# Four tokens to a partition for q and k of the first two units, and the second unit's norms ahead of its gates

## The chip, the cores and the metric

One core of one Trainium2 chip runs the whole kernel. The metric is device time in microseconds of one execution; the median over several runs is compared. The engines are TensorE (PE; PEld is its weight load), VectorE (DVE), ScalarE (ACT), GpSimd (POOL) and SyncE (SP), each with an instruction stream of its own that runs in order; they wait for one another on semaphores. Loads that change float32 to float16 are issued by GpSimd ("software queue"), plain ones by SP or ScalarE ("hardware queue"); all of them share 16 DMA engines.

## What is computed

```python
# q, k, v: (8 batches, 8 heads, 576 tokens, 64), chunks of 64 tokens
scores = scale * q_c @ k_c.T            # within each chunk
attn = softmax(scores)                  # over the chunk's 64 keys
out = attn @ v_c                        # (B, H, S, D)
x = out.transpose(0, 2, 1, 3).reshape(4608, 512)
h = x @ w_in                            # w_in (512, 2048)
g = h * sigmoid(beta * h)               # beta (2048)
y = g @ w_out                           # w_out (2048, 512), output float32
```

## The kernel before, in words

The 4608 tokens are cut into 18 units of 256 tokens (two tiles of 128, four chunks). Two units make a block of 512 tokens, so there are nine blocks. For each unit:

- q and k are loaded with a cast to float16 (`load_qk`, issued on GpSimd, lines 112 to 115), two neighbouring tokens to a partition: partition p holds tokens 2p and 2p+1 of all eight heads, so each row that DMA moves is two tokens of one head, 128 float32 (512 bytes). v is loaded in two tiles of 128 tokens (`load_v`, line 120).
- VectorE transposes 32x32 blocks of 4-byte pairs (`emit_T`, line 164), which puts pairs of the head dimension on partitions. Chunk c of the unit then lies on partitions 32c to 32c+31.
- TensorE makes the scores (`emit_sc`, line 232): for each head, two halves `e` of the head dimension, four chunks, 64 matmuls of 32x64 by 64 columns. ScalarE makes the exponentials into `et` (line 241).
- TensorE multiplies by v (`emit_pv`, line 270), with a column of twos that gives the row sums; the two 128-token halves go to two PSUM tiles. VectorE normalises (`emit_norm`, lines 307 and 313: a reciprocal, then two products per half).
- TensorE transposes x (`emit_xt_pe`, line 329) and ScalarE copies it to SBUF (lines 331 and 333).

Then each block runs the feed-forward part. `emit_m(j, m, ...)` (line 372) makes one group of 128 rows of h from four matmuls; ScalarE takes a tanh (line 384) and VectorE the gate `(tanh + 1) * h` (`emit_mg`, line 360). `emit_t` and `emit_prod` multiply by w_out. The PSUM tiles of `emit_m`, of `emit_xt_pe` and of the idle matmuls below share a pool of four banks (`ps_p`); a tile's bank is free again once its last reader is through. A group of `emit_m` whose gate has not run holds its bank.

The order on each engine is written out by hand (`tc.manual_schedule`): instructions are queued as the program calls them. The start of the kernel, lines 615 to 714, is a list of its own:

- The first unit's q and k come in two halves of four heads: heads 0 to 3 by SP as float32 into `raw0` (cast by ScalarE, line 179, for q, and by VectorE, line 182, for k), heads 4 to 7 by GpSimd. `emit_T_half` and `emit_sc_half` handle one half each.
- GpSimd's queue then goes: v tiles 0 and 1, q and k of the second unit, w_in 0, v tiles 2 and 3, the identity for TensorE's transposes (`make_identity`), w_in 1 to 7, w_out 0 to 2, the third unit's loads, w_out 3, and so on. Eight semaphores take turns for GpSimd's loads, so a load waits until the one eight places ahead has landed.
- `emit_idle(n, w)` (line 612) puts n matmuls of w columns on TensorE that compute nothing needed.
- For the first block the groups m = 0 to 5 are done in two column halves: columns 0 to 255 (the first unit) around the second unit's attention, columns 256 to 511 once its x is there, then m = 6 to 15 in full width.

The gate is done at once after the group unless `gate=False` is given, in which case `emit_mg` is called later.

The functions that the change touches, and what calls them:

Of the kernel before, what the change touches and what calls it, by code (L numbers as in the profile page):

```python
# [8 lines left out]
FP32 = mybir.dt.float32  # L9
FP16 = mybir.dt.float16  # L10
ACTF = mybir.ActivationFunctionType
# [4 lines left out]
def kernel(  # L16
# [10 lines left out]
    nc = tc.nc  # L27
    B, H, S, D = q.shape
# [58 lines left out]
    def runs(t0, n):  # L87
        done = 0
        while done < n:
# [2 lines left out]
            yield done, step, b, s  # L92
            done += step

    q_t = {}
    k_t = {}

    def load_qk(u):
        for src, dst, nm in ((q, q_t, "qu"), (k, k_t, "ku")):
            t = qk_p.tile([128, H, 2, D], FP16, tag=nm, name=nm)  # L100
            if u >= XU:
                dst[u] = t
                tv = t.rearrange("p h r d -> p (h r d)").rearrange("p (s h d) -> p s h d", s=2, h=H)
                for sp in range(2):
                    for off, n, b, s in runs(u * UNIT + sp * 128, 128):
                        nc.gpsimd.dma_start(  # L106
                            out=tv[off:off + n, sp],
                            in_=src[b, :, s:s + n, :].rearrange("h p d -> p h d"),
                        )
                continue  # L110
            for off, n, b, s in runs(u * UNIT, UNIT):
                nc.gpsimd.dma_start(
                    out=t[off // 2:(off + n) // 2],
                    in_=src[b, :, s:s + n, :].rearrange("h (p r) d -> p h r d", r=2),
                )
            dst[u] = t

    def load_v(i):
        for off, n, b, s in runs(i * 128, 128):
            nc.gpsimd.dma_start(  # L120
                out=vbig[off:off + n, i % NV, :, 0:D],
                in_=v[b, :, s:s + n, :].rearrange("h p d -> p h d"),
            )
# [13 lines left out]
    def load_w_in(g):  # L137
        nc.gpsimd.dma_start(
            out=w_in16[g],
            in_=moe_w_in[:, g * 256:(g + 1) * 256].rearrange("(k p) f -> p k f", p=128),  # L140
        )
# [10 lines left out]
    def emit_T(u, which=("kT", "qT")):  # L152
        for nm in which:
            src, dst = {"kT": (k_t, kT), "qT": (q_t, qT)}[nm]
            a = src.pop(u)
            t = qt_p.tile([128, H, CH, 2], FP16, tag=nm, name=nm)
            dst[u] = t
            if u >= XU:
                nc.sync.dma_start_transpose(
                    out=t.rearrange("p h s e -> p (h s e)").rearrange("p (j t) -> p j t", t=128),  # L160
                    in_=a.rearrange("p h r d -> p (h r d)"),
                )
                continue
            nc.vector.transpose(  # L164
                out=t.rearrange("p h s e -> p (h s e)").bitcast(FP32).rearrange(
                    "p (h i r) -> p h r i", h=H, r=2),
                in_=a.rearrange("p h r d -> p (h r d)").bitcast(FP32).rearrange(
                    "p (h r i) -> p h r i", h=H, r=2),
            )
        loads_to(u + 4)  # L170

# [5 lines left out]
    def emit_T_half(a):  # L177
        if a == 0:
            nc.scalar.copy(out=qk0[a][0], in_=raw0[0])
        for i in (0, 1):  # L180
            if a == 0 and i == 1:
                nc.vector.tensor_copy(out=qk0[a][1], in_=raw0[1])
            nc.vector.transpose(
                out=qkT0[a][i].rearrange("p h s e -> p (h s e)").bitcast(FP32).rearrange(
                    "p (h i r) -> p h r i", h=HH, r=2),
                in_=qk0[a][i].rearrange("p h r d -> p (h r d)").bitcast(FP32).rearrange(
                    "p (h r i) -> p h r i", h=HH, r=2),
            )

    def emit_sc_half(a):  # L190
        if a == 0:
            et_t[0] = et_p.tile([128, 2, H, CH], FP16, tag="et", name="et")
            x_t["s0"] = ps_s[0].tile([128, 2, H, CH], FP32, tag="s", name="sc")
        sc = x_t["s0"]
        qt, kt = qkT0[a]
        for h in range(HH):
            for e in range(2):
                for c in range(4):
                    p0, o0 = 32 * c, 64 * (c % 2)
                    nc.tensor.matmul(  # L200
                        out=sc[o0:o0 + 64, c // 2, HH * a + h, :],
                        lhsT=kt[p0:p0 + 32, h, :, e],
                        rhs=qt[p0:p0 + 32, h, :, e],
                        start=(e == 0),
                        stop=(e == 1),
                    )
        hs = slice(HH * a, HH * a + HH)
        nc.scalar.activation(out=et_t[0][:, :, hs], in_=sc[:, :, hs], func=ACTF.Exp, scale=scale)

    def emit_sc(u, split=False):  # L210
        qt, kt = qT.pop(u), kT.pop(u)
        sc = ps_s[0].tile([128, 2, H, CH], FP32, tag="s", name="sc")
        if u >= XU:
            qx, kx = (t.rearrange("p h s e -> p (h s e)").rearrange("p (j c t) -> p j c t", j=H, c=2)
                      for t in (qt, kt))
            for jj in range(H):
                for par in range(2):
                    for c in range(2):
                        nc.tensor.matmul(
                            out=sc[64 * c:64 * c + 64, par, jj, :],  # L220
                            lhsT=kx[64 * par:64 * par + 64, jj, c, :],
                            rhs=qx[64 * par:64 * par + 64, jj, c, :],
                        )
            et = et_p.tile([128, 2, H, CH], FP16, tag="et", name="et")
            nc.scalar.activation(out=et, in_=sc, func=ACTF.Exp, scale=scale)
            et_t[u] = et
            return
        for h in range(H):
            for e in range(2):
                for c in range(4):  # L230
                    p0, o0 = 32 * c, 64 * (c % 2)
                    nc.tensor.matmul(  # L232
                        out=sc[o0:o0 + 64, c // 2, h, :],
                        lhsT=kt[p0:p0 + 32, h, :, e],
                        rhs=qt[p0:p0 + 32, h, :, e],
                        start=(e == 0),
                        stop=(e == 1),
                    )
        et = et_p.tile([128, 2, H, CH], FP16, tag="et", name="et")
        for s in ([0, 1] if split else [slice(0, 2)]):  # L240
            nc.scalar.activation(out=et[:, s], in_=sc[:, s], func=ACTF.Exp, scale=scale)  # L241
        et_t[u] = et

    def emit_pv(u, halves=(0, 1)):
# [17 lines left out]
            return  # L262
        for s in halves:
            i = 2 * u + s
            pool, tag = (ps_x, "x") if s == 0 else (ps_s[0], "s")
            x = pool.tile([128, 2, 4, 128], FP32, tag=tag, name="x")
            for g in range(4):
                for r in range(2):
                    for c in range(2):
                        nc.tensor.matmul(  # L270
                            out=x[64 * c:64 * c + 64, r, g, 0:D + 1],
                            lhsT=et[64 * r:64 * r + 64, s, 4 * c + g, :],
                            rhs=vbig[64 * r:64 * r + 64, i % NV, 4 * c + g, 0:D + 1],
                        )
            x_t[u, s] = x
# [338 lines left out]
    with tc.manual_schedule():  # L614
# [2 lines left out]
        nc.vector.memset(vbig[:, :, :, D:D + 1], 2.0)  # L617
        for a, eng, dst in ((0, nc.sync, raw0), (1, nc.gpsimd, qk0[1])):
            for i, src in enumerate((q, k)):
                eng.dma_start(  # L620
                    out=dst[i],
                    in_=src[0, HH * a:HH * a + HH, 0:UNIT, :].rearrange("h (p r) d -> p h r d", r=2),
                )
        bv = moe_beta.rearrange("(m w f) -> w m f", w=4, f=32)
        for w in range(4):
            nc.sync.dma_start(out=braw[32 * w:32 * w + KFF, :], in_=bv[w])
        load_v(0)
        load_v(1)
        load_qk(1)
        load_w_in(0)  # L630
        load_v(2)
        load_v(3)
        nxt[0] = 2
        make_identity(nc, ident)
        for g in range(1, 8):
            load_w_in(g)
        for g in range(3):
# [2 lines left out]
        load_w_out(3)  # L640
        loads_to(3)

        emit_idle(10, 512)
        emit_T_half(0)
        emit_sc_half(0)
        emit_idle(8, 128)
# [12 lines left out]
        emit_idle(5, 512)  # L659
        emit_T(1)  # L660
        emit_sc(1, True)
        emit_m(0, 0, 0, 256)
        emit_m(0, 1, 0, 256)
        emit_pv(1)
        emit_idle(3, 512)
        emit_norm(1, 0)
        emit_norm(1, 1)
        emit_m(0, 2, 0, 256)
        emit_m(0, 3, 0, 256)
        emit_xt_pe(1, 0)  # L670
        emit_m(0, 4, 0, 256)
        emit_xt_pe(1, 1)
        emit_m(0, 5, 0, 256)
        for m in range(6):
            emit_m(0, m, 256, 256)
# [212 lines left out]
```

## Time and profile before

| | |
|---|---|
| median of 3 runs | 277.3 us (276.9 to 277.51) |
| profiled execution | 277.92 us, its span 276.2 us |
| PE busy | 266.6 us (97% of the span) |
| DVE busy | 210.2 us (76%) |
| ACT busy | 166.7 us (60%) |
| POOL busy | 95.2 us (34%) |
| software queue | 99136 packets, 18.10 MB, 83.7% of 16 engines |
| granted TensorE clock | 1.00 |

Busy time is a share over the whole span. The profile's 40 slices are of 6.9 us each and show by tenths how busy an engine was in each. In the timeline and the groups each line names the engine, the line of the kernel, the operation, what it writes and reads, its shape, how many there were, and in brackets the engine's idle time ahead of it and what ended that. A matmul's duration there includes its way through the array, so neighbouring ones overlap.

### The profile page before, as it was taken

Reading aid. Unit: us, or ns where it says so; the run is one execution under the profiler, and the core shown is the slowest. Engines: PE = TensorE matmul, PEld = TensorE weight load, DVE = VectorE, ACT = ScalarE, POOL = GpSimd, SP = SyncE. Lnnn points to the kernel's source line nnn. Section 1 sums busy time; section 2 is a strip of 40 time slices with the busy share of each in tenths; the row PEclk is TensorE's granted clock in tenths of the full one; section 3 lists DMA queues with packets and bytes.
Section 4 is the critical chain, followed back from the end, with each engine's and each line's share of the span. In section 5 each row is a group of like instructions: output and inputs, shape, how many; then the busy total and the mean of one; then the engine's idle time right before and its main releaser. Section 6 shows DMA issues by size and latency. Waiting matters only on the chain.

```text
span 276.2 us, 7826 instructions
## 1 busy us (share of the span) xinstructions
PE 266.6 (97%) x3238; PEld 185.0 (67%) x3238; DVE 210.2 (76%) x394; ACT 166.7 (60%) x300; POOL 95.2 (34%) x122
## 2 busy tenths in 40 slices
PE   6799999999999999999999999999999999999995
PEld 2565445856756566666666666668887887778874
DVE  3457855899988589767967887659896978787961
ACT  2368515886555566456654656567678495858721
POOL 8854488489539944343445200000000000000000
PEclk9999999999999999999999999999999999999999
DMA  9999999999999999999999999963112102110223
GB/s 141 160 194 202 191 175 179 242 170 165 177 150 144 166 166 171 176 147 146 154 160 193 135 134 195 170 170 81 38 40 76 40 0 78 38 40 1 79 77 114
DMA packets 141763, 36.43 MB, mean 132 GB/s; under 512 B 125856, under 2 KB 141216, under 8 KB 141728
## 3 DMA queue, kind: packets, MB, share of 16 engines
q0 software_dynamic: 99136, 18.10, 83.7%
q1 hardware_dynamic: 42592, 17.84, 34.6%
q8 instruction: 25, 0.41, 0.6%
q14 instruction: 10, 0.08, 0.1%
HBM read 36.71 MB, written 9.44 MB: 167 GB/s over the span
## 4 chain that ended last, share of the span: by engine, by line
PE 64%; DMA 15%; DVE 9%; POOL 5%; ACT 4%; issue 3%; DVEq 0%; ACTq 0%; POOLq 0%
PE hps L372 22%; PE ya L585 14%; PE yb L585 11%; DMA wout<-in_moe_w_out_dram 5%; PE acc L585 5%; PE qx L484 4%; PE qz L484 4%; DMA qu<-in_q_dram 3%; DMA win<-in_moe_w_in_dram 3%; DMA ku<-in_k_dram 3%; ACT hq L513 3%; POOL vbig L120 2%; DVE gt L360 2%; DVE gt L527 2%; DVE sm L436 1%
## 5 line engine op out<-in xcount | busy, mean ns | idle before, releaser
L372 PE MATMUL hps<-xt,win 128*128 128x512 f16 (+1 forms) x488 | 106.6, 355 | 0.7 <-DVE gt L360 0.3
L384 ACT ACTIVATE sg<-hps,bt 128x512 f32<-128x512 f32 (+1 forms) x111 | 69.4, 634 | 36.3 <-PE hps L372 33.8
L360 DVE SCALAR_TENSOR_TENSOR gt<-sg,hps 128x512 f16<-128x512 f32 (+1 forms) x111 | 67.7, 616 | 30.3 <-ACT sg L384 29.4
L372 PEld LDWEIGHTS <-win 128*128 128x128 f16 x488 | 46.2, 98 | 32.8 <-issue 1.0
L585 PEld LDWEIGHTS <-sm 128*128 128x128 f16 x512 | 49.4, 98 | 12.1 <-issue 0.3
L585 PEld LDWEIGHTS <-gt 128*128 128x128 f16 x384 | 36.9, 98 | 10.3 <-DVE gt L527 0.8
L120 POOL DMA_DIRECT2D vbig<-in_v_dram x40 | 33.9, 859 | 26.4 <-PE hps L372 8.2
L585 PE MATMUL ya<-wt,sm 128*128 128x256 f16 x200 | 25.9, 273 | 0.0
L527 DVE TENSOR_SCALAR gt<-hq,rb 128x512 f16<-128x512 f32 x36 | 16.3, 483 | 8.4 <-ACT hq L513 7.2
L106 POOL DMA_DIRECT2D qu<-in_q_dram x20 | 17.0, 864 | 15.6 <-DVE qT L164 6.7
L106 POOL DMA_DIRECT2D ku<-in_k_dram x20 | 17.1, 873 | 10.8 <-DMA qu<-in_q_dram 6.4
L513 ACT ACTIVATE hq<-hq,bs 128x256 f32<-128x256 f32 (+1 forms) x36 | 19.2, 612 | 1.9 <-DVE hq L506 1.9
L436 DVE TENSOR_TENSOR sm<-gt 128x2048 f16<-128x2048 f16 (+1 forms) x17 | 19.7, 1156 | 0.3
L602 ACT COPY osb<-ya 128x512 f32<-128x512 f32 x18 | 10.6, 588 | 8.6 <-PE ya L585 7.9
L484 PEld LDWEIGHTS <-ws 128*128 128x128 f16 x144 | 14.1, 98 | 2.4 <-issue 0.7
L241 ACT ACTIVATE et<-sc 128x1024 f16<-128x1024 f32 (+1 forms) x10 | 8.3, 852 | 11.5 <-PE sc L232 11.5
L397 PE MATMUL ops<-wout,gt 128*128 128x512 f16 x64 | 14.7, 380 | 0.0
L585 PE MATMUL yb<-wout,gt 128*128 128x256 f16 x104 | 13.9, 273 | 0.3 <-DVE gt L527 0.2
L585 PE MATMUL yb<-wt,sm 128*128 128x256 f16 x104 | 13.5, 273 | 0.1
L503 ACT COPY hq<-qx 128x512 f32<-128x512 f32 x18 | 10.5, 586 | 5.0 <-PE qx L484 4.8
L585 PE MATMUL ya<-wout,gt 128*128 128x256 f16 x104 | 13.5, 273 | 0.0
L585 PE MATMUL yb<-wout,sm 128*128 128x256 f16 x104 | 13.5, 273 | 0.0
(99 smaller groups left out, 355.6 us busy)
## 6 DMA issues: line engine op xcount, KB each, us to landing
out_dram<-osb SPq DMA_DIRECT2D x32, 256.0 KB, 2.8
vbig<-in_v_dram POOLq DMA_DIRECT2D x32, 128.0 KB, 7.8
qu<-in_q_dram POOLq DMA_DIRECT2D x18, 128.0 KB, 10.2
ku<-in_k_dram POOLq DMA_DIRECT2D x18, 128.0 KB, 11.2
win<-in_moe_w_in_dram POOLq DMA_DIRECT2D x8, 256.0 KB, 9.5
wout<-in_moe_w_out_dram POOLq DMA_DIRECT2D x4, 512.0 KB, 12.5
qu<-in_q_dram POOLq DMA_DIRECT2D x5, 256.0 KB, 6.6
ku<-in_k_dram POOLq DMA_DIRECT2D x5, 256.0 KB, 7.2
```

Source lines behind the costliest of these rows:

```text
L106: nc.gpsimd.dma_start(out=tv[off:off + n, sp], in_=src[b, :, s:s + n, :].rearrange("h p d -> p h d"),)
L120: nc.gpsimd.dma_start(out=vbig[off:off + n, i % NV, :, 0:D], in_=v[b, :, s:s + n, :].rearrange("h p d -> p h d"),)
L360: nc.vector.scalar_tensor_tensor(out=gt_t[j][:, m, c0:c0 + n], in0=sg[:, 0:n], scalar=1.0, in1=hps[:, 0:n], op0=ALU.add, op1=ALU.mult,)
L372: nc.tensor.matmul(out=hps[:, 0:n], lhsT=w_in16[m // 2][:, kk, (m % 2) * 128:(m % 2) * 128 + 128], rhs=xr[:, c0 // CH:(c0 + n) // CH, 2 * ...
L384: nc.scalar.activation(out=sg[:, 0:n], in_=hps[:, 0:n], func=ACTF.Tanh, scale=bt[:, m:m + 1])
L397: nc.tensor.matmul(out=ops, lhsT=gt_t[j][:, kk, t * 128:(t + 1) * 128], rhs=w_out16[kk // 4][:, kk % 4, :], start=(kk == 0), stop=(kk == K ...
L436: nc.vector.tensor_tensor(out=sm[i][:, lo:hi, :], in0=a, in1=b, op=op)
L484: nc.tensor.matmul(out=dst[:, s, :], lhsT=lhsT, rhs=rhs, start=(p in (1, 2, 5) and s == 0 and kk == 0), stop=(s == 1 and kk == 1), skip_gr ...
L513: nc.scalar.activation(out=o, in_=src, func=ACTF.Silu, scale=bs[:, m:m + 1])
L527: nc.vector.tensor_scalar(out=gt_t[j][:, m, :], in0=hq[:, b].rearrange("p c q -> p (c q)"), scalar1=rb[:, m:m + 1], scalar2=None, op0=ALU. ...
L585: nc.tensor.matmul(out=dst, lhsT=lhsT, rhs=rhs, start=(p in (1, 2, 5) and kk == 0 and (t == 0 or last)), stop=(kk == 7 and (t == 1 or last ...
L602: nc.scalar.copy(out=o, in_=acc)
```

## The change

- `quads` is a new load pattern: partition 64 * (head mod 2) + p holds tokens 4p to 4p+3 of the heads of that parity, so a row is four tokens of one head (1 KB of float32), and each load becomes two, one for each half of the partitions. The first unit's two halves and the second unit use it; other units stay as they are.
- For the first unit's first half, k is issued from ScalarE's queue, q stays on SP. A one-column exponential is put on ScalarE behind those issues.
- `emit_T` and `emit_T_half` transpose with four in place of two tokens to a partition.
- `scores4` replaces the scores of the first two units: the chunks lie on 32 partitions by pair and head parity, the scores go to two PSUM tiles (one for each 128-token half) instead of one, and the exponential is one instruction for each of these. `emit_pv` reads `et` in that order and uses the two PSUM pools the other way round for the first two units.
- The identity is made ahead of v tiles 2 and 3.
- Idle matmuls: 13 in place of 10 at the start, and 3 of 512 columns behind the second unit's p·v are gone.
- The second unit's norms go ahead of the gates of m = 0 and 1, and its transposes stand one place earlier among the groups.

```diff
+    def quads(t, src, h0, nh, t0):
+        tv = t.rearrange("p h r d -> p (h r d)").rearrange("p (h w) -> p h w", h=nh // 2)
+        for hp in range(2):
+            yield (tv[64 * hp:64 * hp + 64],
+                   src[0, h0 + hp:h0 + nh:2, t0:t0 + UNIT, :].rearrange("h (p r) d -> p h (r d)", r=4))
...
+            if u == 1:
+                for out_, in_ in quads(t, src, 0, H, UNIT):
+                    nc.gpsimd.dma_start(out=out_, in_=in_)
+                dst[u] = t
+                continue
...
+            n = 4 if u == 1 else 2
             nc.vector.transpose(
                 out=t.rearrange("p h s e -> p (h s e)").bitcast(FP32).rearrange(
-                    "p (h i r) -> p h r i", h=H, r=2),
+                    "p (h i r) -> p h r i", i=32, r=n),
...
+    def scores4(u, qk, h0, nh):
+        qt, kt = (t.rearrange("p h s e -> p (h s e)").rearrange("p (h s e) -> p h s e", h=nh, e=2) for t in qk)
+        if h0 == 0:
+            et_t[u] = et_p.tile([128, 2, 2, H // 2, CH], FP16, tag="et", name="et")
+            sc4[:] = [pool.tile([128, 2, 4, 128], FP32, tag=tag, name="sc").rearrange(
+                "p b g c -> p b (g c)").rearrange("p b (h q) -> p b h q", q=CH)
+                for pool, tag in ((ps_s[0], "s"), (ps_x, "x"))]
+        for h in range(nh):
+            for c in range(2):
+                for e in range(2):
+                    for s in range(2):
+                        for hp in range(2):
+                            p0, o0 = 64 * hp + 32 * s, CH * c
+                            nc.tensor.matmul(
+                                out=sc4[s][o0:o0 + CH, hp, h0 + h, :],
+                                lhsT=kt[p0:p0 + 32, h, o0:o0 + CH, e],
+                                rhs=qt[p0:p0 + 32, h, o0:o0 + CH, e],
+                                start=(e == 0),
+                                stop=(e == 1),
+                            )
+        for s in range(2):
+            nc.scalar.activation(out=et_t[u][:, s, :, h0:h0 + nh], in_=sc4[s][:, :, h0:h0 + nh], func=ACTF.Exp, scale=scale)
...
-            pool, tag = (ps_x, "x") if s == 0 else (ps_s[0], "s")
+            pool, tag = (ps_x, "x") if (s == 0) == (u > 1) else (ps_s[0], "s")
...
-                            lhsT=et[64 * r:64 * r + 64, s, 4 * c + g, :],
+                            lhsT=(et[64 * r:64 * r + 64, s, g % 2, 2 * c + g // 2, :] if u < 2
+                                  else et[64 * r:64 * r + 64, s, 4 * c + g, :]),
...
-                eng.dma_start(
-                    out=dst[i],
-                    in_=src[0, HH * a:HH * a + HH, 0:UNIT, :].rearrange("h (p r) d -> p h r d", r=2),
-                )
+                for out_, in_ in quads(dst[i], src, HH * a, HH, 0):
+                    (nc.scalar if a == 0 and i else eng).dma_start(out=out_, in_=in_)
...
+        nc.scalar.activation(out=rb[:, 0:1], in_=idle[:, 0:1], func=ACTF.Exp)
         load_v(0)
         load_v(1)
         load_qk(1)
         load_w_in(0)
+        make_identity(nc, ident)
         load_v(2)
         load_v(3)
         nxt[0] = 2
-        make_identity(nc, ident)
...
-        emit_idle(10, 512)
+        emit_idle(13, 512)
...
         emit_T(1)
         emit_sc(1, True)
-        emit_m(0, 0, 0, 256)
-        emit_m(0, 1, 0, 256)
+        emit_m(0, 0, 0, 256, gate=False)
+        emit_m(0, 1, 0, 256, gate=False)
         emit_pv(1)
-        emit_idle(3, 512)
         emit_norm(1, 0)
         emit_norm(1, 1)
+        emit_mg(0, 0)
+        emit_mg(0, 1)
+        emit_xt_pe(1, 0)
         emit_m(0, 2, 0, 256)
         emit_m(0, 3, 0, 256)
-        emit_xt_pe(1, 0)
+        emit_xt_pe(1, 1)
         emit_m(0, 4, 0, 256)
-        emit_xt_pe(1, 1)
         emit_m(0, 5, 0, 256)
```

More of the change, by code (lines that the diff above doesn't have):

```diff
@@ L163, in emit_T @@
                 continue
+            n = 4 if u == 1 else 2
             nc.vector.transpose(
                 out=t.rearrange("p h s e -> p (h s e)").bitcast(FP32).rearrange(
-                    "p (h i r) -> p h r i", h=H, r=2),
+                    "p (h i r) -> p h r i", i=32, r=n),
                 in_=a.rearrange("p h r d -> p (h r d)").bitcast(FP32).rearrange(
-                    "p (h r i) -> p h r i", h=H, r=2),
+                    "p (h r i) -> p h r i", i=32, r=n),
             )
@@ L184, in emit_T_half @@
                 out=qkT0[a][i].rearrange("p h s e -> p (h s e)").bitcast(FP32).rearrange(
-                    "p (h i r) -> p h r i", h=HH, r=2),
+                    "p (h i r) -> p h r i", i=32, r=4),
                 in_=qk0[a][i].rearrange("p h r d -> p (h r d)").bitcast(FP32).rearrange(
-                    "p (h r i) -> p h r i", h=HH, r=2),
+                    "p (h r i) -> p h r i", i=32, r=4),
             )
-    def emit_sc_half(a):
[L191 to L205, printed above, removed]
-                    )
-        hs = slice(HH * a, HH * a + HH)
-        nc.scalar.activation(out=et_t[0][:, :, hs], in_=sc[:, :, hs], func=ACTF.Exp, scale=scale)
@@ L210, in emit_sc @@
+    sc4 = []
+    def emit_sc_half(a):
+        scores4(0, qkT0[a], 2 * a, 2)
     def emit_sc(u, split=False):
         qt, kt = qT.pop(u), kT.pop(u)
+        if u == 1:
+            scores4(1, (qt, kt), 0, H // 2)
+            return
         sc = ps_s[0].tile([128, 2, H, CH], FP32, tag="s", name="sc")
@@ L619 @@
             for i, src in enumerate((q, k)):
-                eng.dma_start(
-                    out=dst[i],
-                    in_=src[0, HH * a:HH * a + HH, 0:UNIT, :].rearrange("h (p r) d -> p h r d", r=2),
-                )
+                for out_, in_ in quads(dst[i], src, HH * a, HH, 0):
+                    (nc.scalar if a == 0 and i else eng).dma_start(out=out_, in_=in_)
         bv = moe_beta.rearrange("(m w f) -> w m f", w=4, f=32)
```

## The prediction, on record before the run

> **What bounds the kernel now.** I read the 40 slices first, to see whether TensorE ever has room.
>
> ```profile
> PE   6799999999999999999999999999999999999995
> PEclk9999999999999999999999999999999999999999
> ```
>
> After the second slice TensorE is full and at full clock. In the trace its waits after 20.25 us come to under 2 us, none of them on a load. So the end can move only if the start of the gapless stretch moves, and the change touches only what lies before it. The waits of the first 20.25 us name the candidates (what waited, for what: us, times, longest).
>
> ```profile
> DVE kT L164 <- DMA ku<-in_k_dram: 1.5, 1, 1.5
> PE x L270 <- DMA vbig<-in_v_dram: 0.9, 1, 0.9
> PEld L372 <- DMA win<-in_moe_w_in_dram: 0.8, 2, 0.6
> ```
>
> Third, the timeline (start, us, engine, line, operation).
>
> ```profile
> 9.83 0.32 PE L270 MATMUL x<-vbig,et 64*64 64x65 f16 x16 [0.89 <-DMA vbig<-in_v_dram]
> 12.67 1.24 PE L612 MATMUL warm<-wt 128*128 128x512 f16 x5
> 12.68 0.71 DVE L164 STREAM_TRANSPOSE kT<-ku 128x512 f32<-128x512 f32 x1 [1.48 <-DMA ku<-in_k_dram]
> ...
> 14.04 0.70 PE L232 MATMUL sc<-qT,kT 32*64 32x64 f16 x64
> ...
> 16.29 0.78 DVE L360 SCALAR_TENSOR_TENSOR gt<-sg,hps 128x256 f16<-128x256 f32 x2 [2.30 <-ACT sg L384]
> 17.00 0.20 DVE L307 RECIPROCAL rd<-x 128x8 f32<-128x8 f32 x1
> 17.11 0.77 PEld L372 LDWEIGHTS <-win 128*128 128x128 f16 x8 [0.58 <-DMA win<-in_moe_w_in_dram]
> ...
> 18.81 1.19 DVE L360 SCALAR_TENSOR_TENSOR gt<-sg,hps 128x256 f16<-128x256 f32 x3
> ...
> 19.62 0.58 ACT L333 COPY xt<-xp 128x512 f16<-128x512 f16 x1
> ...
> 20.25 0.49 PE L372 MATMUL hps<-xt,win 128*128 128x256 f16 x3 [0.24 <-ACT xt L333]
> ```
>
> Two stretches set 20.25. **A**, up to the second unit's scores at 14.04: TensorE would have come to them at about 13.77 (five idle matmuls behind the first unit's last transposes, a string that hangs on the second v tile's landing at 9.79), but q's transpose ended at 13.99, since k of that unit landed at 12.66. **B**, from 14.04 to 20.25, 6.21 us: scores, p·v, then VectorE does two gates before the norms, and the last norm, transpose, ScalarE copy of x end at 20.20. Twelve groups (m 0 to 5, both column halves) need only w_in 0 to 2, and half of them stand before 20.25 in both kernels; so each us off 20.25 is a us off the end, if later data comes in time.
>
> **The change, part by part.**
>
> *GpSimd's issues.* Four loads become eight. An issue costs 0.60 and 0.58 us for 256 rows of 512 bytes (third unit's 32-partition pieces), 0.77 for 768 and 0.87 to 0.93 for 1024: about 0.5 + 0.0004 a row. Now rows are 1 KB: 128 a load for the first unit (estimate 0.55, between 0.5 and the 0.89 of the very first issue), 256 for the second (0.59). First unit's half: 0.89 + 0.76 = 1.65 becomes 0.7 + 3 x 0.55 = 2.35; the second unit's pair: 1.8 becomes 2.4. So the v issues start 0.7 later, the second unit's last k issue at 7.1 instead of 5.47, w_in 0 at 7.7 instead of 6.34; with the identity (0.67) now ahead of two v loads, w_in 1 at 10.9 instead of 9.44.
>
> *What DMA gets for that.* The software queue is behind, so landings come in order and at the engines' pace: 1.41 and 1.46 us for q and k of the second unit (1024 rows of 512 bytes), 0.83 for a v tile, 1.36 and 1.31 for w_in tiles (512 rows of 1 KB). A q or k load in 1 KB rows has a w_in tile's rows, so 1.33: the pair saves 0.2 and the first unit's half about 0.05. The pace is that of the slowest of 16 engines; the fastest had the v tile at 7.41, 3.67 after its issue, the slowest at 9.79 (the trace counts landings engine by engine), because its backlog came from the first loads. With half as many rows ahead of it I put the v landing at 9.6 (bounds 9.0, if the backlog is all rows, and 10.5, if it follows the issue, 0.7 later). Then k at 9.6 + 2 x 1.33 = 12.25 at that pace and no earlier than 7.1 + 3.65 = 10.75 at the fastest engine's; I take 12.15, bounds 11.3 and 13.8. w_in 1 at k + 1.35 + 2 x 0.83 + 1.34 = 16.5, against 17.06.
>
> *First half on two hardware queues.* q from SP and k from ScalarE's queue, two issues each of about 0.46 (SP's row), so both land near 4.1 instead of 3.81 and 5.05. VectorE's string there (transpose 0.45, cast 0.70, transpose 0.45) then ends at 6.2 to 6.4 as before. ScalarE's table load (1.28) moves behind its two issues and ends at about 3.0, ahead of q. If this half came 1 us late, the scores would be at 7.3, p·v still by 9.8: the v wait covers it. Cost nothing.
>
> *Scores by parity.* Same 64 matmuls a unit, four row groups at a time into four banks; groups of four start every 32 ns now and should again. The first unit's exponential of 512 (597 ns) becomes two of 256. From 597 at 512 and 1.02 us at 1024 one of 256 is 0.39, and the second starts 0.28 behind, so each half's pair ends 0.07 later. Both are under the v wait. Thirteen idle matmuls for ten end at about 5.9, ahead of the first scores.
>
> *A, summed.* TensorE's string gives 13.77 - 0.19 = 13.58; the loads give 12.15 + 0.02 + 1.33 (two transposes) + 0.05 = 13.55. Scores at 13.6: 0.45 earlier (bounds 12.9 and 15.1).
>
> *B, re-run with its own rows.* p·v of the first half ends 1.93 behind the scores' start (15.98 - 14.04), VectorE's norms can start at 15.58, as the gates are behind them now: 1.9 us for both halves (17.00 to 18.89), ending at 17.47. First gate 17.8, second 18.14. TensorE transposes x of the first half at 16.6, copy on ScalarE 16.95 to 17.53; m2 at 16.7 to 17.1 (w_in 1: 16.5; a landing up to 17.2 costs nothing, since m3 needs a PSUM bank that this copy frees). m3 17.58, second transposes 18.02 (their bank: first gate), m4 18.24 (second gate), m5 18.68. ScalarE: tanh of m3 to 18.68, copy of x 18.62 to 19.20, gapless from 19.25. So B takes 5.65 instead of 6.21: 0.55. The three idle matmuls taken out (0.82) are part of this, and so is the new wait: the gates' banks hold up m3 and m4 until 17.53 and 18.14, behind which the second transposes queue, and that is in the sum.
>
> *The rest.* From 19.25 the order is the old one. Margins at 1.0 earlier: w_in 3 lands at 20.32 and is needed at 21.9; w_out 0 27.86 and 30.5; w_out 3 40.14 and 42.1; the third unit's scores at 38.4, its q transpose ends at 37.3. None binds.
>
> **Sum**: 0.45 + 0.55 = 1.0 us off. The profiled execution took 277.92 (span 276.2, 1.7 around it): 276.9. The median of the runs, 277.3, is 0.6 below it, so on that scale **276.3 us**. A measurement here tells about 0.2%, 0.55 us, from nothing.
>
> **Rivals.**
>
> *The v tile follows its issue.* GpSimd reaches it 0.7 later; if it lands at 10.5, TensorE's string gives scores at 14.45, and B's 5.65 leads to 20.1: 0.15 gained, 277.15. For it: the fastest engine did follow the issue (3.65 and 3.67 us for the two v tiles). Against: the landing is the slowest's, 2.4 us later. 0.12.
>
> *Slower: eight issues starve the second unit.* If every small issue costs the 0.89 of the first one, its last k load is issued at 1.25 + 4 x 0.89 + 1.75 + 3 x 0.89 = 9.23, and with the 4.53 from issue to landing of the first unit's k it lands at 13.76 at best; with the 7.2 that the second unit's took, at 16.4. Scores at 15.1 to 17.8, gapless from 20.8 to 23.4: 277.85 to 280.5, say 278.2. It decides from a k landing at 13.2 (loss of all gain) and 13.75 (a loss to be seen). Against: 0.58 measured for 256 rows. 0.13.
>
> *Transposes at a wider step.* VectorE's transposes now write 4-byte elements 16 bytes apart, 8 before. The trace has only 8 (446 ns for 256 elements, 671 to 712 for 512: 0.95 an element and 0.2 fixed) and contiguous (168 for 32, no faster than that by much), so 16 may cost nothing or double. Doubled, the second unit's two end at 12.15 + 0.02 + 2.66 = 14.83, gapless from 20.5: 277.55; the first unit's lie under the v wait. 0.07. The Trainium skill, "SBUF — State Buffer", section "Door 1: The DMA port swizzle", says that SBUF has 16-byte lines and that full speed needs at least two hits in one. By that rule the new step has one hit and would pay; no trace here shows it yet, and the 8-byte rows agree with both.
>
> *The gain is eaten later* by a load that does not move (VectorE waits 1.56 us for the third unit's k at 35.99): 277.3. Its scores start 2 us behind the transposes, more than the shift. 0.03.
>
> **How the numbers follow.** Forecast 0.65, nearly all of it over 0.55 us gained (0.55 comes from B alone). With the few better ends of the rivals, faster by over 0.2% 0.68; within 0.2% 0.18 (v tile, wide step, eaten gain, a small part of the forecast); slower 0.14 (the starved unit, and the end of the wide step). Range: the early end has scores at 12.9 (gain 1.7) and run to run 0.2, 275.4; the late end takes in the v tile and the doubled transposes, 277.7. Left out are most of the slower rival and the far early tail, under 2 in 10. The forecast's own range is 275.5 to 276.8.
>
> **What would show it.** Right: second-unit scores between 13.2 and 13.9, norms ahead of the gates with no VectorE work between p·v and them, first gapless matmul at 18.8 to 19.6, and every later wait shifted by one amount. Wrong: TensorE waiting on vbig past 10.2, or VectorE on ku past 13.2; transposes well over 0.71 us; score matmuls over 0.70 us a unit; or a gapless start that moves and an end that does not.

## The result, and the profile after

| | before | after |
|---|---|---|
| median | 277.37 us (6 runs, 276.9 to 277.68) | 279.49 us (6 runs, 278.88 to 279.69) |
| ratio to before | | 1.0074, 95% interval 1.0061 to 1.0087 |
| profiled execution (span) | 277.92 (276.2) | 279.42 (277.6) |
| granted TensorE clock, mean | 1.00 | 0.994 |

The change is slower by 2.05 us (1.7 to 2.4); 276.3 was forecast. The 40 slices of after answer to those of before:

```profile
PE   6789999999999999999999999999999999999995
PEclk9799999999999999999999999999999999999999
```

One more slice has room, and the second slice (6.9 to 13.9 us) now has a granted clock of 0.7. The waits that matter are no longer those of before (what waited, for what: us, times, longest):

```profile
ACT sm L191 <- DMA sm<-in_q_dram: 2.5, 1, 2.5
...
PE sc L215 <- DVE sm L195: 2.4, 1, 2.4
```

TensorE's waits for v and for w_in and VectorE's for the second unit's k are gone. In their place ScalarE waits 2.5 us for the first unit's q, and TensorE 2.4 us for what follows from it. Rows of the timeline of after (start, us, engine, line, operation, idle time before and what ended it; here and below rows between those shown are left out):

```profile
0.74 1.37 ACTq L645 DMA_DIRECT2D sm<-in_k_dram  x2
0.74 1.63 SPq L645 DMA_DIRECT2D sm<-in_q_dram  x2
...
6.17 0.62 ACT L191 CAST sm<-sm 128x512 f16<-128x512 f32 x1 [2.52 <-DMA sm<-in_q_dram]
...
8.42 0.46 PE L215 MATMUL sc<-sm 32*64 32x64 f16 x32 [2.42 <-DVE sm L195]
8.81 1.03 PE L636 MATMUL warm<-wt 128*128 128x128 f16 x8
10.16 1.03 PE L636 MATMUL warm<-wt 128*128 128x128 f16 x8
11.13 0.65 PE L293 MATMUL x<-vbig,et 64*64 64x65 f16 x32
...
13.44 1.09 DVE L176 STREAM_TRANSPOSE kT<-ku 128x512 f32<-128x512 f32 x1
14.37 1.07 DVE L176 STREAM_TRANSPOSE qT<-qu 128x512 f32<-128x512 f32 x1
15.49 0.70 PE L215 MATMUL sc<-qT,kT 32*64 32x64 f16 x64
17.48 0.21 DVE L331 RECIPROCAL rd<-x 128x8 f32<-128x8 f32 x1 [2.04 <-PE x L293]
19.30 1.07 DVE L384 SCALAR_TENSOR_TENSOR gt<-sg,hps 128x256 f16<-128x256 f32 x3
19.50 0.60 PE L396 MATMUL hps<-xt,win 128*128 128x256 f16 x4 [0.24 <-ACT xt L357]
...
49.71 0.26 PE L293 MATMUL x<-vbig,et 64*64 64x65 f16 x9 [0.45 <-issue]
```

The same stretch of before, for comparison:

```profile
0.74 0.46 SPq L620 DMA_DIRECT2D sm<-in_q_dram  x1
...
3.83 0.62 ACT L179 CAST sm<-sm 128x512 f16<-128x512 f32 x1 [1.81 <-DMA sm<-in_q_dram]
...
6.31 0.45 PE L200 MATMUL sc<-sm 32*64 32x64 f16 x32 [1.10 <-DVE sm L183]
...
6.69 0.62 PE L612 MATMUL warm<-wt 128*128 128x128 f16 x8
```

Read downwards, the timeline of after shows nearly the whole loss of this execution.

- The first unit's q is issued in two pieces of about 0.8 us each (1.63 for two, 0.46 for the whole q before). The second lands at 6.08, so the cast starts at 6.17 and the first scores at 8.42, where they were at 6.31.
- The eight idle matmuls behind them take 1.03 us at 8.81 and again at 10.16, where eight of this size at full clock take 0.62: TensorE has been slowed.
- p·v of the first unit starts at 11.13 with no wait for v, which had landed at 8.26 and 9.12. k of the second unit had landed at 12.54, but VectorE is at the first unit's norms until 13.5.
- The transposes take 1.09 and 1.07 instead of 0.71 and 0.67, and the second unit's scores stand at 15.49, where they were at 14.04.
- From there part B does as forecast: reciprocal (norms) at 17.48, ahead of the gates at 19.30. The w_out stage starts at 32.38 (31.50 before), so only 0.88 of the 1.45 us is left.
- At 49.71, in the middle of the fourth unit's p·v and behind no wait that the profile shows, TensorE stalls for 0.45 us. From there on everything is about 1.35 late.

### The profile page after: what moved, and what is told of

The parts are those of the page before. It is cut to its first block, busy times and chain, and to the rows that moved or that the text cites. A ratio compares the mean times of both kernels' runs of the same rounds, so it can differ in the third digit from the quotient of the medians.

```text
span 277.6 us, 7844 instructions
## 1 busy us (share of the span) xinstructions
PE 267.1 (96%) x3238; PEld 185.6 (67%) x3238; DVE 210.4 (76%) x394; ACT 167.2 (60%) x303; POOL 96.9 (35%) x126
## 4 chain that ended last, share of the span: by engine, by line
PE 75%; DVE 11%; DMA 5%; ACT 4%; issue 2%; POOL 1%; SPq 0%; DVEq 0%; ACTq 0%
PE hps L396 27%; PE ya L609 14%; PE yb L609 11%; PE acc L609 5%; PE qx L508 4%; PE qz L508 4%; PE ops L421 3%; DMA qu<-in_q_dram 3%; DVE gt L384 2%; ACT hq L537 2%; DVE gt L551 2%; DMA sm<-in_q_dram 2%; DVE x L337 2%; DVE sm L460 1%; PE warm L636 1%
## 5 line engine op out<-in xcount | busy, mean ns | idle before, releaser
L609 PE MATMUL yb<-wout,gt 128*128 128x256 f16 x104 | 13.9, 273 | 0.2
L609 PE MATMUL yb<-wt,sm 128*128 128x256 f16 x104 | 13.5, 273 | 0.1
L609 PE MATMUL ya<-wout,gt 128*128 128x256 f16 x104 | 13.5, 273 | 0.0
L609 PE MATMUL yb<-wout,sm 128*128 128x256 f16 x104 | 13.5, 273 | 0.0
L264 ACT ACTIVATE et<-sc 128x1024 f16<-128x1024 f32 (+1 forms) x8 | 7.2, 917 | 10.1 <-PE sc L255 10.1
```

What stands on the lines that cost most here:

```text
L609: nc.tensor.matmul(out=dst, lhsT=lhsT, rhs=rhs, start=(p in (1, 2, 5) and kk == 0 and (t == 0 or last)), stop=(kk == 7 and (t == 1 or last ...
```

## The experiments

Theory: (1) the first unit's half that comes by two hardware queues in pieces is the loss, with TensorE's clock behind it; the part with the norms is sound. Rival (2): the second unit's half of the new layout, with its slower transposes, is the loss.

All results in one table. "Scores" are the starts of the first unit's first scores and of the second unit's in the profiled execution; ratios are to the kernel before on the same chip, with 95% intervals.

| kernel | scores, us | median, us | ratio |
|---|---|---|---|
| before | 6.31, 14.04 | 277.4 | |
| after | 8.42, 15.49 | 279.49 | 1.0074 (1.0061 to 1.0087) |
| after_again | 8.97, 16.44 | 280.23 | 1.0097 (1.0073 to 1.0121) |
| b_only | 5.57, 13.39 | 276.65 | 0.9976 (0.9966 to 0.9987) |
| u0_old | 6.07, 13.64 | 276.74 | 0.9986 (0.9966 to 1.0006) |
| u1_old | 8.28, 15.84 | 279.32 | 1.0068 (1.0052 to 1.0084) |
| clk | 8.48, 14.87 | 278.73 | 1.0046 (1.0028 to 1.0063) |
| wide | 5.57, 14.17 | 277.81 | 1.0012 (1.0003 to 1.0021) |
| split64 | 10.98, 18.39 | 282.25 | 1.0169 (1.0150 to 1.0187) |
| half2 | 9.01, 16.38 | 280.69 | 1.0129 (1.0102 to 1.0156) |
| heads2 | 6.32, 13.22 | 277.62 | 1.0003 (0.9976 to 1.0029) |
| half2_late | 7.84, 15.41 | 279.12 (one run) | |
| act_q | 6.35, 14.00 | 277.15 | 0.9987 (0.9975 to 0.9998) |
| sp_only | 8.01, 15.29 | 279.00 | 1.0057 (1.0043 to 1.0071) |
| nat2 | 5.70, 12.96 | 277.25 | 0.9996 (0.9982 to 1.0011) |
| nat4 | 5.65, 15.36 | 277.01 | 0.9989 (0.9975 to 1.0004) |
| b_qfirst | 5.49, 12.61 | 276.58 | 0.9974 (0.9959 to 0.9990) |

### Which part loses

**b_only**, the kernel before with the new order of norms and gates alone:

```diff
-        emit_m(0, 0, 0, 256)
-        emit_m(0, 1, 0, 256)
+        emit_m(0, 0, 0, 256, gate=False)
+        emit_m(0, 1, 0, 256, gate=False)
         emit_pv(1)
-        emit_idle(3, 512)
         emit_norm(1, 0)
         emit_norm(1, 1)
+        emit_mg(0, 0)
+        emit_mg(0, 1)
+        emit_xt_pe(1, 0)
         emit_m(0, 2, 0, 256)
         emit_m(0, 3, 0, 256)
-        emit_xt_pe(1, 0)
-        emit_m(0, 4, 0, 256)
         emit_xt_pe(1, 1)
+        emit_m(0, 4, 0, 256)
         emit_m(0, 5, 0, 256)
```

> The kernel before with the last part of the change alone: the second unit's norms ahead of its two gates, its transposes one place earlier, the three idle matmuls behind its p·v gone. Loads, layout and transposes are those of before. Theory 1 (this part is sound and worth what it was forecast): scores of the second unit still at 14.0, gapless stretch from 19.7 instead of 20.25, 0.55 us off the end, about 276.8. Rival (what is won at the start is given back later, by a load or by an instruction stall like the 0.45 us gap at 49.7 of the changed kernel): gapless from 19.7, end 277.3 or later.

Measured 276.65, 0.67 us off (0.36 to 0.94). Its timeline:

```profile
8.14 0.67 PE L270 MATMUL x<-vbig,et 64*64 64x65 f16 x32
...
12.04 0.71 DVE L164 STREAM_TRANSPOSE kT<-ku 128x512 f32<-128x512 f32 x1 [1.39 <-DMA ku<-in_k_dram]
...
13.39 0.70 PE L232 MATMUL sc<-qT,kT 32*64 32x64 f16 x64 [0.71 <-DVE qT L164]
...
15.38 0.21 DVE L307 RECIPROCAL rd<-x 128x8 f32<-128x8 f32 x1 [2.04 <-PE x L270]
...
17.39 0.60 PE L372 MATMUL hps<-xt,win 128*128 128x256 f16 x4 [0.24 <-ACT xt L333]
```

The first line matters for all that follows: p·v of the first unit runs at 8.14 without waiting for v, and the path is the second unit's k (landed 12.01). The profiled execution of before, with its wait for v until 9.83, had its loads later than most. What the new order is worth is best read from the second unit's scores to one later wait of TensorE, ahead of a later unit's scores (65.73 in before, 64.39 here). The distance is 51.38 to 51.69 us with the old order (before, act_q, wide, split64, half2, half2_late), and 51.00 to 51.13 with the new one (b_only, u0_old, clk, u1_old, sp_only, after_again): 0.5 us. Five traces do not price the order: in heads2 (52.04) and b_qfirst (51.81), with the earliest scores of each order, TensorE then waits for v or w_in, after has its stall in this stretch, and in nat2 and nat4 the scores themselves take longer.

**u0_old** is the changed kernel with the first unit loaded, transposed and scored as before, **u1_old** the same for the second unit. The main edit of u0_old:

```diff
-                for out_, in_ in quads(dst[i], src, HH * a, HH, 0):
-                    (nc.scalar if a == 0 and i else eng).dma_start(out=out_, in_=in_)
+                eng.dma_start(
+                    out=dst[i],
+                    in_=src[0, HH * a:HH * a + HH, 0:UNIT, :].rearrange("h (p r) d -> p h r d", r=2),
+                )
```

With it, `emit_T_half`, `emit_sc_half` and the first unit's index into `et` are those of before.

> The changed kernel with the first unit loaded, transposed and scored as before (both first loads on SP, two tokens to a partition); the second unit keeps four tokens to a partition. Theory 1 (the late first-unit loads, and TensorE's slowed clock behind the wait for them, are the loss): first scores back at 6.3, no wait of 2.4 us, full clock; then the second unit's k (landing about 12.5) and its two transposes of 1.08 set its scores at about 14.6, gapless from 20.3, 277.4, 2 us less than the changed kernel. Rival 2 (the second unit's half of the layout is the loss): stays near 279.3, with the second unit's scores at 15.4.

> The changed kernel with the second unit loaded, transposed and scored as before; the first unit keeps the new loads. Theory 1 (first unit's late loads): first scores still at 8.4 behind a wait of 2.4 us; the second unit's transposes take 0.7 each instead of 1.08, but TensorE's own string reaches that unit's scores at about 15.4 anyway, so 279.3, at most 0.2 less than the changed kernel. Rival 2 (second unit's wide transposes and loads): 277.4 to 277.8, scores of the second unit near 14.0.

u0_old came to 276.74, 2.75 below the changed kernel; u1_old to 279.32, 0.17 below it. Rival 2 falls: the first unit's part is the whole loss, and once it is that late, the second unit's transposes at 0.70 instead of 1.08 change nothing, as VectorE and TensorE come to them late anyway. With the first unit as before, the second unit's new layout is worth about nothing: u0_old against b_only is 276.74 to 276.65. u0_old came 0.7 below its forecast, which had taken over after's k landing at about 12.5. Here k landed at 11.48 (12.01 in b_only) and its two transposes took 2.06 instead of 1.35 from start to scores; the loads' gain is eaten by the transposes.

**clk**, the changed kernel with more idle matmuls ahead of the first scores:

```diff
-        emit_idle(13, 512)
+        emit_idle(22, 512)
```

> The changed kernel with 22 idle matmuls of 512 columns at the start instead of 13, so that TensorE is busy until about 8.0 and idles 0.4 us instead of 2.4 ahead of the first scores at 8.42. Nothing else is changed. Theory 1 with the clock (the wait itself lets the granted clock fall, so the idle matmuls behind the first scores take 1.03 us instead of 0.62): both strings back at 0.62, p·v of the first unit at about 10.7 instead of 11.13, 0.4 off the end, about 279.0. Rival (the low clock costs nothing, as other work ends last): no change, 279.5.

Measured 278.73, with a granted clock of 1.00:

```profile
8.77 0.62 PE L636 MATMUL warm<-wt 128*128 128x128 f16 x8
...
14.87 0.71 PE L215 MATMUL sc<-qT,kT 32*64 32x64 f16 x64
```

The first scores are as late as in after (8.48 against 8.42), but the idle matmuls are back at 0.62, and the second unit's scores come 0.6 earlier. Six of clk's seven executions have a granted clock of 0.999 or 1.00, and all six of after have 0.994. So about 0.8 us of the loss (1.0074 to 1.0046, intervals that just overlap) is the clock that TensorE loses by the wait; 0.4 was forecast. The two strings of idle matmuls alone are 0.41 longer each in after. The rest is the lateness itself.

The Trainium skill, "TensorE: Matmul & The Clock Gate", section "Part 1: The HAM clock gate (the "warmup" mystery)", says that the array runs at half its clock after an idle window of about 3.4 us, and that these windows run freely, so that the moment differs from run to run. The half, the length and the shifting moment agree with the traces. From start to start these idle matmuls are 107 ns apart in after and 56 ns in clk. The granted clock of after is 0.50 from 8.35 to 11.77 us and 1.00 before and behind; in after_again, nat4 and u1_old it is 0.50 for as long, from 9.93, 11.19 and 10.46. That the window is idle throughout does not agree: in the 3.41 us ahead of the slow stretch TensorE was busy for 1.06 us in after, for 1.71 in nat4, where it had waited 1.23 for v, and for 2.09 in u1_old. In nat4 five idle matmuls of 512 columns then took 2.13 us instead of 1.24. Waits of 1.30 (heads2) and 1.48 (wide) brought no slow stretch, with 1.92 and 1.93 us busy in their windows; so busy time alone does not tell which short wait costs, and these runs leave that open.

### Why the first unit's loads land late

**split64**, and then **half2** and **heads2**, put pieces into the kernel before without the new layout (rows of 512 bytes, two tokens to a partition). split64:

```diff
+                if a == 0:
+                    for hp in range(2):
+                        (nc.scalar if i else eng).dma_start(
+                            out=dst[i][64 * hp:64 * hp + 64],
+                            in_=src[0, 0:HH, 128 * hp:128 * hp + 128, :].rearrange("h (p r) d -> p h r d", r=2),
+                        )
+                    continue
```

> The kernel before with one thing changed: the first unit's first half is loaded as in the changed kernel by halves of the partitions, q in two DMAs from SP and k in two from ScalarE's queue, but with the rows of before (512 bytes, two tokens to a partition). Theory 1a (two queues and 64-partition pieces make the late landing): the second pieces land at 5.5 to 6.1, first scores at 7.5 to 8, p·v of the first unit up to 1 us later, 277.6 to 278.3. Rival 1b (the 1 KB rows, or GpSimd's own 64-partition loads beside them, make it): all landed by 5.0, first scores at 6.3 or earlier, 277.4.

The second pieces landed at 6.77 and 7.51, later than in after and than the 5.5 to 6.1 of theory 1a, so the 1 KB rows are not to blame. At 282.25 the run is 4 us past both forecasts, as it held a second cost besides:

```profile
7.59 1.28 ACT L179 ACT_TABLE_LOAD   x1 [7.59 <-DMA sm<-in_q_dram]
```

With DMA issues on its queue, ScalarE's table load had gone behind the wait for q. The changed kernel avoids that by its one-column exponential. half2 is split64 with that exponential; heads2 has the same number of pieces, bytes and rows, but cut by heads, each over all 128 partitions:

```diff
-                            out=dst[i][64 * hp:64 * hp + 64],
-                            in_=src[0, 0:HH, 128 * hp:128 * hp + 128, :].rearrange("h (p r) d -> p h r d", r=2),
+                            out=dst[i][:, 2 * hp:2 * hp + 2],
+                            in_=src[0, 2 * hp:2 * hp + 2, 0:UNIT, :].rearrange("h (p r) d -> p h r d", r=2),
```

> The kernel before with the first unit's first half in two pieces each by partition halves, q on SP and k on ScalarE's queue (512-byte rows), and the one-column exponential behind the issues, so that ScalarE's table load no longer stands between q's landing and its cast. Theory 1e (pieces, however cut, land late since GpSimd's loads get onto the engines before the second pieces do): second pieces at 6 to 7.5 as in the run without the exponential, table load done by 3.5, first scores at 8.5 to 9.5, 279.5 to 281.

> The same, but with the pieces cut by heads: two heads a piece over all 128 partitions, the same rows, bytes and number of DMAs. Theory 1e (the second issue is what comes late): second pieces at 5.5 to 7.5, first scores at 7.5 or later, 278.3 or more. Rival 1f (a piece on 64 partitions is slow, whatever its turn): second pieces by 5.0, first scores by 6.5, 277.4.

half2's timeline, and then heads2's:

```profile
0.74 1.38 ACTq L622 DMA_DIRECT2D sm<-in_k_dram  x2
0.74 1.64 SPq L622 DMA_DIRECT2D sm<-in_q_dram  x2
...
7.07 0.62 ACT L179 CAST sm<-sm 128x512 f16<-128x512 f32 x1 [3.43 <-DMA sm<-in_q_dram]
```

```profile
0.74 1.05 ACTq L622 DMA_DIRECT2D sm<-in_k_dram  x2
0.74 0.98 SPq L622 DMA_DIRECT2D sm<-in_q_dram  x2
...
4.38 0.62 ACT L179 CAST sm<-sm 128x512 f16<-128x512 f32 x1 [1.06 <-DMA sm<-in_q_dram]
```

Theory 1e (any second piece is late) falls, and 1f stands: cut by heads, the second pieces landed at 4.30 and 4.59 and the kernel is as fast as before; cut by partitions they landed at 6.99 and 6.76, and it is 3.6 us slower. A piece over 64 partitions costs 0.63 to 0.84 us of issue, one over 128 costs 0.46 to 0.53.

**half2_late** puts two memsets ahead of GpSimd's loads in half2, so that those start 1.27 us later:

```diff
+        for n in range(2):
+            nc.gpsimd.memset(wt[n].rearrange("p a b -> p (a b)").bitcast(FP32), 0.0)
```

> The kernel with the partition halves, with two memsets of other tiles put on GpSimd ahead of its loads, so that those start 1 to 3 us later. All that hangs on GpSimd's loads then comes later too, so only the landings of the first half's four pieces are of interest. Theory 1e (GpSimd's loads crowd the second pieces out): second pieces 1 us or more earlier than with the halves alone, by 5.0. Rival 1f (slow by themselves): no earlier, 6 or more.

The second pieces landed at 5.71 and 5.52 instead of 6.99 and 6.76: 1.25 us earlier, though not by 5.0. So both hold a share, as far as one profile of each can say: against heads2, about half of the 2.4 us goes when GpSimd's loads come later, and half stays. Why a piece over 64 partitions is slow by itself, no run here shows.

**act_q** leaves q and k whole and puts k on ScalarE's queue, with the exponential; **sp_only** is the changed kernel with all four pieces on SP:

```diff
-                eng.dma_start(
+                (nc.scalar if a == 0 and i else eng).dma_start(
```

```diff
-                    (nc.scalar if a == 0 and i else eng).dma_start(out=out_, in_=in_)
+                    eng.dma_start(out=out_, in_=in_)
```

> The kernel before with the first unit's first k on ScalarE's queue and q on SP, each still one DMA over all 128 partitions in 512-byte rows, and the one-column exponential behind the issue so that ScalarE's table load does not wait for q. Theory 1c (splitting by partition halves makes the late landing: each piece costs 0.70 to 0.83 us of issue instead of 0.46, and the second piece's packets start only when GpSimd's are on the engines): both land by 4.2, first scores at 5.5, 277.4 or up to 0.3 less. Rival 1d (two hardware queues side by side make it): landings of 5.5 or later, first scores at 7 or later, 277.6 to 278.3.

> The changed kernel with all four first loads of its first half on SP, k's two pieces behind q's two. Theory 1c (the pieces' issues of about 0.75 each make it): q's second piece as late as before the edit or 0.5 earlier (5.5 to 6.1), k's second piece issued at 3.0 and landing at 6.5 to 7.5; first scores at 8.5 to 9.2, 279.5 to 280.3. Rival 1d (the second queue makes it): q by 4.8, k by 5.5, first scores at 7.0 to 7.3, 278.2.

act_q: q landed at 4.39 and k at 4.88, so 1d falls for whole loads: two queues do no harm that the time shows, but no good either (3.45 to 3.81 for q, and 4.28 to 5.05 for k, where both were on SP). 1c's landings by 4.2 and first scores at 5.5 were missed too. Why it is 0.36 us faster (0.05 to 0.7) its trace doesn't say: its second unit's scores stand at 14.00. sp_only missed both forecasts: first scores at 8.01, 279.00. q's second piece came at 5.20, 0.9 earlier than with two queues, and k's last, though third and fourth in line, was cast at 6.86. So with pieces the second queue seems to cost too, 0.5 us against after, which is within the noise, and 1.2 against after_again on the same chip, which is not.

The Trainium skill, "DMA: Bandwidth & Descriptors", section "Rules for kernel authors", advises against two transfers to disjoint halves of the partitions, as they share the same engines either way, and says that spreading DMAs over SP, ScalarE and GpSimd brings no bandwidth. half2 against heads2 (2.4 us of landing) and act_q against before agree with the advice. The reason given, shared engines, does not tell why heads2's pieces, as many and as large, landed earlier.

### The transposes

**wide** is the kernel before with only the step of the second unit's transposes changed:

```diff
-                    "p (h i r) -> p h r i", h=H, r=2),
+                    "p (h i r) -> p h r i", i=32, r=4 if u == 1 else 2),
```

> The kernel before with one thing changed: the second unit's two transposes write their 4-byte elements 16 bytes apart instead of 8 (the data are then out of order, so that the output is not the reference's; sizes, instructions and loads are the same). Theory 1 (the step alone prices the transposes): 1.08 us each instead of 0.71 and 0.67, and both lie on the path to the second unit's scores, so 0.75 later there and at most 0.75 at the end: 277.9 to 278.2. Rival (the slower transposes of the changed kernel come from something else, such as a clash with DMA writes or with TensorE's reads): 0.7 each and no change, 277.4.

```profile
12.13 1.08 DVE L164 STREAM_TRANSPOSE kT<-ku 128x512 f32<-128x512 f32 x1 [1.74 <-DMA ku<-in_k_dram]
13.07 1.05 DVE L164 STREAM_TRANSPOSE qT<-qu 128x512 f32<-128x512 f32 x1
14.17 0.70 PE L232 MATMUL sc<-qT,kT 32*64 32x64 f16 x64 [1.48 <-DVE qT L164]
```

The durations are those of after, with only the output's step changed (the input is read in the same order): the step alone is the price, 0.37 us for 512 elements, and the rival falls. At the end it is 0.33 us (0.08 to 0.58), less than forecast and about half of what the two transposes add; where the other half goes is not shown.

**nat2** (on b_only) and **nat4** (on u0_old) go the other way and write q's transpose to adjoining elements, with the tokens picked by the matmul. nat2:

```diff
+            if u == 1 and nm == "qT":
+                nc.vector.transpose(
+                    out=t.rearrange("p h s e -> p (h s e)").bitcast(FP32),
+                    in_=a.rearrange("p h r d -> p (h r d)").bitcast(FP32),
+                )
+                continue
...
+            qt = qt.rearrange("p h s e -> p (h s e)").rearrange("p (h r i e) -> p h i r e", h=H, r=2, e=2)
...
-                        rhs=qt[p0:p0 + 32, h, :, e],
+                        rhs=qt[p0:p0 + 32, h, ..., e],
```

> The kernel with the norms ahead of the gates (276.65) and one thing more: the second unit's q is transposed to adjoining elements (4 bytes apart instead of 8), and the score matmuls pick its tokens by a two-step pattern of their moving operand. If the time of a transpose goes by the step of what it writes (0.7 at 8 bytes, 1.08 at 16), q's takes about 0.5 and the scores come 0.2 earlier: 276.45. If 8 bytes is already at full speed: 0.67 and no change. If the moving pattern is slow: score matmuls over 0.70 us a unit, and later.

> The changed kernel with the first unit as before (276.74) and one thing more: the second unit's q is transposed to adjoining elements instead of 16 bytes apart, and the score matmuls pick its tokens by a two-step pattern. If a transpose goes by its step: q's takes 0.5 instead of 1.05, the second unit's scores come at 13.1 instead of 13.64, 276.2 to 276.3, ahead of all others. If the moving pattern is slow: score matmuls over 0.70 us, and 276.7 or later.

```profile
12.23 0.67 DVE L165 STREAM_TRANSPOSE qT<-qu 128x512 f32<-128x512 f32 x1
12.96 1.30 PE L240 MATMUL sc<-qT,kT 32*64 32x64 f16 x64
```

A step of 4 bytes is no faster than one of 8 (0.67 both); 16 bytes is the one that costs, and nat4's q took 0.68 instead of 1.05. But the moving operand with two steps makes the 64 score matmuls take 1.30 us instead of 0.70 (1.11 in nat4), which eats what it brings: no gain in either. The profiled execution of nat4 took 278.93, 1.9 over its median; its wait for v and the half clock behind it, both told above, belong to that execution, and the other eleven have a clock of 0.998 or more.

### The late stall, and a faster version

**after_again** is the changed kernel unaltered.

> The changed kernel once more, for a second profile of it. The stall of 0.45 us in the middle of the fourth unit's p·v at 49.7, behind no wait that the profile shows, was in none of the traces of its variants. If it belongs to one execution: gone here, and the end follows the start of the gapless stretch by the same distance as in the variants (about 258.4 us from the last wait of 0.24 us to the end). If it belongs to this kernel: there again at the same matmul.

```profile
49.67 0.61 PE L293 MATMUL x<-vbig,et 64*64 64x65 f16 x32
```

The same 32 matmuls without a gap: the stall is not a fixed part of this kernel. What the profile's 0.45 us were, stays open. The 258.4 us of the expectation was a slip; the distance from the last 0.24 us wait to the end is 259.1 to 259.5 in b_only, u0_old, u1_old, clk and sp_only, and 259.3 here (20.45 to 279.76). This execution lost its time before that: first scores at 8.97.

**b_qfirst** is b_only with q's transpose ahead of k's:

```diff
-        emit_T(1)
+        emit_T(1, ("qT", "kT"))
```

> The kernel with the norms ahead of the gates and one thing more: of the second unit's two transposes q's goes first. q landed at 10.56 there and k at 12.01, and VectorE waited 1.39 us for k while q lay ready; so q's 0.67 moves into that wait, k's ends at 12.75, scores at 12.8 instead of 13.39, where TensorE's own string (idle matmuls to 12.68) is next: 0.55 off 276.65, 276.1. Rival (the string or a v tile is later in most executions): 276.4 to 276.65.

```profile
12.61 0.71 PE L232 MATMUL sc<-qT,kT 32*64 32x64 f16 x64
...
13.71 1.05 PE L372 MATMUL hps<-xt,win 128*128 128x256 f16 x8 [0.39 <-DMA win<-in_moe_w_in_dram]
```

The scores come at 12.61, 0.8 earlier than in b_only, and the end doesn't move (276.58 against 276.65): TensorE next waits for w_in 0, which landed at 13.67, and for 0.6 us in all on the w_in loads. The rival was right that the gain is lost, but wrong on where. b_only and b_qfirst are faster than both kernels of this case: 0.7 us off before, 2.9 off after.

## Why the prediction was wrong

**The step that failed: "First half on two hardware queues".** It put both loads near 4.1 by pricing each piece's issue with SP's 0.46 for a whole load, and costed the edit at nothing. The pieces cost 0.6 to 0.8 each and landed at 6.08 and 5.75. half2 and heads2 show the cause: pieces on 64 partitions, not their number. About half of the delay goes with GpSimd's loads coming later (half2_late); the second queue may add 0.5 to 1.2 us (sp_only). The prediction weighed the Trainium skill's rule on the step and not its rule on halves of the partitions, quoted above, which spoke against this edit.

**The cover that was named did not exist.** "If this half came 1 us late, the scores would be at 7.3, p·v still by 9.8: the v wait covers it" was read from one execution, in which the second v tile landed at 9.79. In the eight other traces with v issued at the same time and no load ahead of it cut by partitions it landed at 8.29 to 9.46, and only nat4's, the 9.46, shows TensorE waiting for it. The first scores stood at 5.49 to 6.35 there. So the half was later by 2.1 to 2.9 us than in these, all of it on the path: p·v, which began between 7.74 and 8.51 there, began at 11.13. This is also why the medians differ by 2.1 us and the profiled executions by 1.5: that of before was 0.55 above its median.

**A term that was missing: TensorE's clock.** The 13 idle matmuls were timed to end "ahead of the first scores". With those late, the wait of 2.4 us brought half clock, 0.8 us by clk.

**Transposes.** The priced term (as before) was wrong, the rival at 0.07 right in kind: 1.08 is 1.5 to 1.6 times the old duration. Its size on the path, and that the first unit's lie "under the v wait", were wrong with the cover: the four of the first unit took 0.61 to 0.63 instead of 0.44 to 0.45, two of them ahead of the first scores. The Trainium skill's rule in "SBUF — State Buffer", section "Door 1: The DMA port swizzle", on two hits to a 16-byte line, is borne out by wide, which changes nothing but the step; 4 and 8 bytes at the same 0.67 agree with it too.

**What held.** B: forecast 0.55, measured 0.5 from the traces and 0.67 (0.36 to 0.94) by b_only. The slower rival (the second unit starved by eight issues) did not happen: GpSimd's small issues cost 0.61 to 0.72 (0.55 and 0.59 forecast), k landed at 12.54, inside its bounds, and v at 9.12. Of those two nothing in after waited. w_in 1 landed at 17.49, 1.0 later than forecast, without effect, since all else was later.

**The sum.** A came to +1.45 in the profiled executions instead of -0.45, B to -0.55 as forecast, the stall to +0.45: 1.35 of the 1.5. The rest, and the stall, are not explained.

## What to carry to other kernels

If a load like these must be cut, cut it by the free dimension and not by the partitions, and price a new shape of DMA by a row of that shape, or from both sides, even when it looks like work that another wait hides. A cover read from one execution is only as good as that execution: landings early in this kernel moved by 1 us or more from run to run, so ask what the path is when the covering wait is not there. When TensorE may wait ahead of a serial stretch, the wait can cost twice, once itself and once in the clock behind it, and idle matmuls that reached up to the work bought the second part back here.

## What the runs showed of the hardware

- The same DMA bytes and rows (heads2, half2): 0.46 to 0.53 us of issue on SP's or ScalarE's queue over 128 partitions, 0.63 to 0.84 over 64; the second pieces of the latter land 2.4 us later beside GpSimd's loads.
- TensorE's granted clock falls to half for a stretch of 3.41 us at a time (after, nat4, u1_old and others; two in a row in split64), and a wait of 1.23 us was enough in one execution (nat4), one of 1.48 not in another (wide).
- A VectorE transpose of 512 4-byte elements takes 0.67 to 0.71 us with its output 4 or 8 bytes apart (nat2, nat4, before) and 1.05 to 1.10 at 16 (wide, after, u0_old, nat4).
- A moving operand of two steps nearly doubled the time of 64 small score matmuls, 0.70 to 1.30 us (nat2).
- VectorE's cast of k (128x512) took from 0.38 to 0.70 us in different executions of the same instruction; no run here says why.
- ScalarE's table load (1.28 us) ran at 0.74 in before, where nothing stands ahead of the first activation, and at 7.59 in split64, behind that activation's wait, where DMA issues stand before it.
